# A gated linear attention with a mixture of experts behind it: the first place done in halves, and two edits to the loads and the order of step 0

## The chip, the cores and the metric

The kernel runs on one core of a Trainium2 chip. The core has a matrix engine (TensorE, PE in the profile, its weight loads PEld), a vector engine (VectorE, DVE), an engine for functions of single elements (ScalarE, ACT), a general one (GpSimd, POOL), and a queue engine (SyncE, SP) that here only issues DMA transfers. ScalarE and GpSimd issue some transfers too. Each engine takes its own instructions in order and waits for others by semaphores. The metric is the time of one execution on the device in microseconds.

## The reference

Inputs q, k, v and alpha have the shape (4 batches, 8 heads, 768 positions, 48). For each batch and head a state of 48 x 48 runs over the positions:

```
state = alpha_t[:, None] * state + k_t (outer) v_t
y_t   = q_t @ state
```

The outputs of all heads at one position are joined to a row x of 384 numbers (3072 rows). Then each row goes to the one of 8 experts with the largest logit:

```
logits = x @ w_gate;  e = argmax(logits);  g = softmax(logits)[e]
out    = g * (relu(x @ w1[e]) @ w2[e])          # w1[e]: 384 x 1024, w2[e]: 1024 x 384
```

All numbers are float32.

## The kernel before

**Places.** The positions are cut into 6 chunks of 128, and each chunk of each batch is a place: 24 places, place s being chunk s // 4 of batch s % 4. Within a place the running products of alpha are taken as exponentials of sums of logarithms. For a place s this happens:

- `load` (L401) issues the transfers of alpha, k, q and v for the place on SP's queue. At the start they go one by one, in the order of the strings in `singly` (L622): each letter is the next transfer of that input.
- `logs` (L411): ScalarE takes the logarithm of alpha (`lna`).
- `cums` (L427): TensorE multiplies `lna` with a triangular matrix, which gives the running sums in the PSUM bank `cum`; ScalarE takes two exponentials of them, `icp` (negative sign) and `cp`. For the two first places the second call takes the bank `x`.
- `operands` (L475): k times `icp` and q times `cp` go into one of three buffers `kqb`. GpSimd does this, and VectorE for place 0.
- `transposes` (L484): TensorE turns four pairs of heads of k, then of q; VectorE or ScalarE copies the result out as `kT` and `qT`.
- `scores` (L498): eight matmuls into the banks `sA` and `sB`.
- `mask` (L507): VectorE multiplies both banks with a causal mask (`dA`, `dB`).
- `attend` (L534): the masked scores with v into `y`; from chunk 1 on `read_state` adds the part of the state before it.
- `keys_values` (L543): k with v into another part of the banks of `y`; `add_state` (L561) copies it out as the batch's state.
- `result` (L555) copies y out as `yT`; `rows` (L570), `logits`, `gate` and `keep_rows` make the row of x, the gate and its weight, and write x to DRAM.
- `decay_out` (L443) sends one row of `cp` or `icp` to another tile with a small DMA, issued on ScalarE's queue.

**Order.** The order of all instructions is written out by hand: the loop over i from -4 to 23 (from L720) calls these functions for different places. Step i takes the scores of place i, the transposes of place i + 1, the operands of place i + 2, and the sums of places that `sums_to` (L612) lists: places 0 and 1 in step -2, places 2 and 3 in step 0, 4 and 5 in step 1, then one or two more per step, until they are five places ahead. The steps before 0 fill the pipeline: `operands(0)` in step -2, `transposes(0)` in step -1. In steps 0 to 2 the second sums stand between `attend` and `keys_values`.

Ahead of the loop, `idle(3)` (L637) issues three matmuls of zeros from the tile `er` whose results are not used.

PSUM has eight banks: two for `y`, two for `tp`, and one each for `cum`, `sA`, `sB` and `x`.

**Experts.** After the last step the rows are sorted to the experts, gathered by indirect DMA, and go through both layers, expert by expert, with weights loaded ahead. The change does not touch this part.

Of the kernel before, what the change touches and what calls it, by code (L numbers as in the profile page):

```python
# [8 lines left out]
F32 = mybir.dt.float32  # L9
# [5 lines left out]
AF = mybir.ActivationFunctionType  # L15
# [5 lines left out]
def kernel(  # L21
# [31 lines left out]
    C = 128  # L53
# [335 lines left out]
    with tc.tile_pool(name="ld", bufs=6) as ld, \  # L389
# [37 lines left out]
        def cums(s, bank="cum"):  # L427
            cum = ps.tile([C, 512], F32, name="cum", tag=bank)
            if s < APART:
                nc.tensor.matmul(cum[:, :Dm], lhsT=cum_m[:], rhs=st[s]["lna"][:], start=True, stop=True)  # L430
# [5 lines left out]
            nc.scalar.activation(icp[:], cum[:, :Dm], AF.Exp, scale=-1.0)  # L436
            nc.scalar.activation(cp[:], cum[:, :Dm], AF.Exp)
            st[s]["cp"], st[s]["icp"] = cp, icp
# [22 lines left out]
        def by_half(t):  # L461
            return t.rearrange("s p a d -> s a p d")[:, :, :, :D]
# [11 lines left out]
        def operands(s):  # L474
            d = st[s]  # L475
            kq = kqb[s % 3]
            eng = nc.gpsimd if s else nc.vector
            for i, n, e in ((0, "k", "icp"), (1, "q", "cp")):
                eng.tensor_tensor(  # L479
                    by_half(kq[:, i]), d[n].rearrange("s (a p) d -> s a p d", a=2),  # L480
                    d[e][:].rearrange("s (a p d) -> s a p d", a=2, p=NP), op=ALU.mult,
                )

        def transposes(s):  # L484
            d = st[s]
            for i, n in enumerate(("kT", "qT")):
                tp = ps.tile([C, NP, C], F32, name="tp", bufs=2)
                for p in range(NP):
                    nc.tensor.transpose(tp[:, p, :], pair(kqb[s % 3][:, i], p), ident[:])  # L489
                d[n] = work.tile([C, NP, C], F32, name=n)  # L490

                if 0 < s < B - 1 or i and s < NT - B - 2:
                    nc.vector.tensor_copy(d[n][:], tp[:])  # L493
                else:
                    nc.scalar.copy(d[n][:], tp[:])
# [109 lines left out]
        def do(f, i, *a):  # L605
            if 0 <= i < NT:
                f(i, *a)
# [12 lines left out]

        loaded = dict(a=0, k=0, q=0, v=0)

        singly = {-5: "aakq", -4: "kqav", -3: "akq", -2: "aav", -1: "kq", 0: "avakq", 1: "avkq", 2: "a"}

        def load_next(n, many):
            load(loaded[n], n, many)
# [2 lines left out]
        def loads_for(i):  # L629
            for n in singly.get(i, ""):  # L630
                load_next(n, 1)
            if i > 1:
                for n, upto in ("a", sums_to(i + 4 + (i > 3))), ("v", i + 3), ("k", i + 5), ("q", i + 5):
                    while loaded[n] <= min(upto, NT - 1):
                        load_next(n, 2)

        def idle(n):  # L637

            t = ps.tile([C, NP, C], F32, name="sA")
            for _ in range(n):  # L640
                nc.tensor.matmul(t[:, :2, :], lhsT=er[:, 0].rearrange("s a d -> s (a d)"), rhs=er[:, :2], start=True, stop=True)

        loads_for(-5)
        nc.vector.memset(er[:], 0.0)
        nc.gpsimd.memset(iw[:], 0.0)
        for i in range(2):
# [66 lines left out]
        for i in range(-4, NT):  # L713
            loads_for(i)
            do(scores, i)
            if i < NT - 1:
                do(result, i - 1)
            do(logits, i - 2)
            if i >= B:
                do(add_state, i - 1)  # L720
            do(gate, i - 2)
            if i > 0:
                for s in new_logs(i):
                    logs(s)
# [676 lines left out]
```

## Time and profile before

Three runs gave a median of 393.21 us (391.83 to 393.31). The profiled execution took 390.48 us; its span is 388.8 us at a granted clock of 0.998.

| | us |
|---|---|
| median of the runs | 393.21 |
| the profiled execution / its span | 390.48 / 388.8 |
| TensorE busy | 380.0 |
| ScalarE / VectorE / GpSimd busy | 230.2 / 210.4 / 149.7 |
| scores of step 0 / 1 begin | 8.95 / 14.08 |

How to read the profile: a timeline line has the start in us, the duration, the engine, the line of the kernel, the operation, what it writes and reads, and the number of instructions merged. In square brackets stands how long the engine was idle before it and what ended that. `SPq` and `ACTq` are DMA issues on these engines' queues. In the rows of digits each digit is the busy share, in tenths, of one fortieth of the span.

### The profile page before, as it was taken

The numbers are of one execution on the slowest core, as the hardware profiler recorded it, in microseconds if no ns is written. First come the engines' busy times: TensorE is split into PE (matmuls) and PEld (weight loads), VectorE is DVE, ScalarE is ACT, GpSimd is POOL, SyncE is SP. The second block draws the span as 40 slices with busy tenths as digits, with TensorE's granted clock in tenths as the row PEclk, the third lists the DMA queues.
The fourth block names the chain that finished last, engine by engine and source line by source line (L and its number), as shares of the span: only waits on it lengthen the run. The fifth ranks groups of instructions, "written<-read, shape, count | busy, mean of one in ns | idle before, by whom it ended". The sixth has DMA issues, their size and how long they took to land. (4 is left out here: it accounts for less than half of the span.)

```text
span 388.8 us, 9126 instructions
## 1 busy us (share of the span) xinstructions
PE 380.0 (98%) x3394; PEld 326.1 (84%) x3394; DVE 210.4 (54%) x649; ACT 230.2 (59%) x521; POOL 149.7 (39%) x203
## 2 busy tenths in 40 slices
PE   7999999999999999999999999999999999999995
PEld 4678888888888886899889979979979979979964
DVE  5554667676676666625843672582581582551200
ACT  4575777677665431545665775675765765763640
POOL 6557464789768203257050034025016012011032
PEclk9999999999999999999999999999999999999999
DMA  9999998998994315789959459758767966701211
GB/s 172 197 205 218 194 227 190 210 220 212 237 260 139 117 42 183 157 293 256 278 154 256 78 194 231 159 187 193 196 195 178 205 195 152 176 16 58 57 55 66
DMA packets 156546, 68.09 MB, mean 175 GB/s; under 512 B 139339, under 2 KB 150722, under 8 KB 156500
## 3 DMA queue, kind: packets, MB, share of 16 engines
q1 hardware_dynamic: 151396, 57.77, 63.2%
q0 software_dynamic: 3408, 9.64, 8.2%
q8 instruction: 28, 0.46, 0.5%
q10 hardware_dynamic: 1696, 0.08, 0.3%
q14 instruction: 18, 0.15, 0.1%
HBM read 49.00 MB, written 9.58 MB: 151 GB/s over the span
## 5 line engine op out<-in xcount | busy, mean ns | idle before, releaser
L1077 POOL DMA_INDIRECT out_dram<-zo,sp x25 | 26.0, 1041 | 136.5 <-ACT zo L1102 127.1
L479 POOL TENSOR_TENSOR kqb<-k_sb,icp 128x384 f32<-128x384 f32 x23 | 23.0, 1000 | 28.7 <-PE y L550 12.5
L1051 PE MATMUL tp<-h_sb,w 128*128 128x416 f32 (+5 forms) x96 | 33.9, 496 | 0.0
L502 PE MATMUL sA<-qT,kT 48*128 48x128 f32 x192 | 27.7, 284 | 0.9 <-DVE qT L493 0.9
L502 PE MATMUL sB<-qT,kT 48*128 48x128 f32 x192 | 27.7, 285 | 0.0
L372 POOL DMA_INDIRECT xg<-x_rows,gp x25 | 23.8, 953 | 10.0 <-issue 6.6
L489 PE MATMUL tp<-ident,kqb 128*128 128x128 f32 x192 | 26.4, 280 | 0.3 <-DVE kqb L479 0.3
L1051 PEld LDWEIGHTS tp<-h_sb,w 128*128 128x128 f32 x96 | 18.0, 190 | 10.3 <-issue 3.7
L502 PEld LDWEIGHTS sA<-qT,kT 48*128 48x128 f32 x192 | 23.1, 187 | 3.8 <-issue 1.1
L980 ACT ACTIVATE h_sb<-h_sb 128x208 f32<-128x208 f32 (+6 forms) x28 | 10.3, 366 | 25.3 <-DVE h_sb L192 24.5
L192 DVE TENSOR_TENSOR h_sb<-cum,u 128x208 f32<-128x208 f32 (+6 forms) x28 | 10.1, 360 | 27.2 <-PE cum L969 20.7
L479 POOL TENSOR_TENSOR kqb<-q_sb,cp 128x384 f32<-128x384 f32 x23 | 23.1, 1003 | 3.1 <-DMA q_sb<-in_q_dram 3.1
L192 DVE TENSOR_TENSOR h_sb<-sB,u 128x208 f32<-128x208 f32 (+6 forms) x28 | 10.1, 360 | 26.1 <-PE sB L969 18.7
L558 ACT COPY yT<-y 128x512 f32<-128x512 f32 x24 | 14.1, 586 | 16.5 <-PE y L550 9.1
L489 PEld LDWEIGHTS tp<-ident,kqb 128*128 128x128 f32 x192 | 20.5, 141 | 3.4 <-issue 0.8
L969 PE MATMUL tp<-xgT,w 128*128 128x208 f32 (+6 forms) x112 | 23.1, 329 | 0.0
L502 PEld LDWEIGHTS sB<-qT,kT 48*128 48x128 f32 x192 | 23.1, 187 | 0.0
L510 DVE TENSOR_TENSOR dA<-sA,cmask 128x512 f32<-128x512 f32 x24 | 16.5, 688 | 10.8 <-PE sB L502 10.6
L195 DVE TENSOR_TENSOR th<-h_sb,th 128x208 f32<-128x208 f32 (+5 forms) x48 | 17.3, 361 | 8.0 <-ACT h_sb L982 8.0
L881 ACT COPY xgT<-xt 128x768 uint16<-128x768 uint16 (+6 forms) x25 | 20.8, 922 | 0.5 <-DMA xt<-xh 0.5
L576 PE MATMUL x<-iw,yT 128*64 128x104 f32 x368 | 20.8, 255 | 0.1
L1102 ACT COPY zo<-zr 128x768 uint16<-128x768 uint16 (+2 forms) x20 | 19.9, 1052 | 0.0
(304 smaller groups left out, 1032.2 us busy)
## 6 DMA issues: line engine op xcount, KB each, us to landing
w<-in_moe_w_dram SPq DMA_DIRECT2D x14, 1536.0 KB, 7.9
x_rows<-xs SPq DMA_DIRECT2D x24, 192.0 KB, 3.7
v_sb<-in_v_dram SPq DMA_DIRECT2D x10, 384.0 KB, 4.8
k_sb<-in_k_dram SPq DMA_DIRECT2D x9, 384.0 KB, 6.3
q_sb<-in_q_dram SPq DMA_DIRECT2D x9, 384.0 KB, 5.9
a_sb<-in_alpha_dram SPq DMA_DIRECT2D x7, 384.0 KB, 4.3
a_sb<-in_alpha_dram SPq DMA_DIRECT2D x10, 192.0 KB, 3.7
w<-in_moe_w_dram SPq DMA_DIRECT2D x6, 256.0 KB, 3.7
```

The source lines that it names most:

```text
L192: eng.tensor_tensor(out, a, b, op=ALU.add)
L195: eng.tensor_tensor(out, a, b, op=ALU.subtract)
L372: nc.gpsimd.indirect_dma_start(out=g["xg"][:r, j, :], out_offset=None, in_=x_d[:, :], in_offset=bass.IndirectOffsetOnAxis(ap=g["gi"](j, r) ...
L479: eng.tensor_tensor(by_half(kq[:, i]), d[n].rearrange("s (a p) d -> s a p d", a=2), d[e][:].rearrange("s (a p d) -> s a p d", a=2, p=NP), ...
L489: nc.tensor.transpose(tp[:, p, :], pair(kqb[s % 3][:, i], p), ident[:])
L502: nc.tensor.matmul(t[:, p, :], lhsT=d["kT"][r : r + D, p, :], rhs=d["qT"][r : r + D, p, :], start=True, stop=True,)
L576: nc.tensor.matmul(d["x"][o : o + HC, m, : D2 + E], lhsT=d["yT"][:, m // 2, m % 2, o : o + HC], rhs=iw[:, m, :], start=True, stop=True,)
L881: nc.scalar.copy(to[:, :, :, j * C : j * C + r], g["xt"][:, j].rearrange("p (h a) t -> p h a t", h=2)[:, :, :, :r],)
L969: nc.tensor.matmul(out, lhsT=ops[n_][0], rhs=ops[n_][1], start=first and n_ == names[0], stop=True, skip_group_check=True,)
L1051: nc.tensor.matmul(d2[:, :n], lhsT=w2[:, f, 2 * C :], rhs=h[:, f, :n], start=(f == 0), stop=(f == FB - 1),)
L1077: ins = nc.gpsimd.indirect_dma_start(out=out[:, :], out_offset=bass.IndirectOffsetOnAxis(ap=g["si"](j, r), axis=0), in_=zo[:r], in_offset= ...
L1102: copy(zo[:r].bitcast(U16).rearrange("p (c h) -> p h c", h=2), g["zr"][:r, j].rearrange("p (h a) c -> p h (a c)", h=2),)
```

## The change

Place 0 gets a function of its own, `first_step`, called in step -2. It takes the sums of place 0 in two halves of 192 columns (pairs of heads 0 and 1, then 2 and 3) in the banks `cum` and `sB`, the sums of place 1 in `x`, the exponentials, the products with k and q, the transposes and the copies of place 0 by halves; `kT` is copied by ScalarE, `qT` by VectorE. The second half of q is turned in the bank `cum`. The exponential `icp` of place 1 stands ahead of the copies of `kT`, `cp` behind them. The calls for place 0 in `cums`, `operands` and `transposes` fall away.

`idle` issues two matmuls of 512 columns instead of three of 256, from a constant zero instead of `er`, and stands ahead of the memsets. In `singly` the string of step -2 has v of place 1 ahead of the sixth transfer of alpha instead of behind it. In step 0 `keys_values` stands ahead of the second sums.

```diff
-        singly = {..., -2: "aav", ...}
+        singly = {..., -2: "ava", ...}
...
         def idle(n):
-            t = ps.tile([C, NP, C], F32, name="sA")
+            t = ps.tile([C, NP * C], F32, name="sA")
+            z = nc.const_aps.tensor(0.0, (C, NP * C))
             for _ in range(n):
-                nc.tensor.matmul(t[:, :2, :], lhsT=er[:, 0].rearrange("s a d -> s (a d)"), rhs=er[:, :2], start=True, stop=True)
+                nc.tensor.matmul(t[:], lhsT=z[:, :C], rhs=z, start=True, stop=True)
+
+        def first_step():
+            d = st[0]
+            two = (slice(0, 2), slice(2, NP))
+            def heads(t, h):
+                return t.rearrange("s (a p d) -> s a p d", a=2, p=NP)[:, :, two[h]]
+            cum = [ps.tile([C, 512], F32, name=n)[:, : Dm // 2] for n in ("cum", "sB")]
+            for h in range(2):
+                nc.tensor.matmul(cum[h], lhsT=cum_m[:], rhs=heads(d["lna"][:], h), start=True, stop=True)
+            one = ps.tile([C, 512], F32, name="x")[:, :Dm]
+            nc.tensor.matmul(one, lhsT=cum_m[:], rhs=st[1]["lna"][:], start=True, stop=True)
...
+            for t, f in zip(by, (-1.0, 1.0)):
+                for h in range(2):
+                    nc.scalar.activation(t[h], cum[h], AF.Exp, scale=f)
...
+            for i, n in enumerate("kq"):
+                t = d[n + "T"] = work.tile([C, NP, C], F32, name=n + "T")
+                for h in range(2):
+                    if i and h:
+                        tp = ps.tile([C, NP, C], F32, name="cum")
+                    elif h == 0:
+                        tp = ps.tile([C, NP, C], F32, name="tp", bufs=2)
+                    tps.append((t[:, two[h]], tp[:, two[h]], nc.vector.tensor_copy if i else nc.scalar.copy))
+                    nc.vector.tensor_tensor(
+                        by_half(kqb[0][:, i])[:, :, two[h]], d[n].rearrange("s (a p) d -> s a p d", a=2)[:, :, two[h]],
+                        by[i][h], op=ALU.mult,
+                    )
+                    for p in range(2 * h, 2 * h + 2):
+                        nc.tensor.transpose(tp[:, p, :], pair(kqb[0][:, i], p), ident[:])
...
+            nc.scalar.activation(st[1]["icp"][:], one, AF.Exp, scale=-1.0)
+            for t, tp, copy in tps:
+                copy(t, tp)
+            nc.scalar.activation(st[1]["cp"][:], one, AF.Exp)
 
         loads_for(-5)
+        idle(2)
         nc.vector.memset(er[:], 0.0)
...
         first_consts()
-        idle(3)
...
         for i in range(-4, NT):
...
-            do(transposes, i + 1)
+            if i >= 0:
+                do(transposes, i + 1)
             sums = list(new_sums(i))
-            for s in sums[:1]:
-                cums(s)
-            if i < 0:
-                for s in sums[1:]:
-                    cums(s, "x")
+            if i == -2:
+                first_step()
+            else:
+                for s in sums[:1]:
+                    cums(s)
...
-            do(operands, i + 2)
+            if i > -2:
+                do(operands, i + 2)
...
+            if i == 0:
+                keys_values(i)
             if i >= 0 and sums[1:]:
                 cums(sums[1])
                 for s in sums:
                     decay_out(s, (0,) if i else (0, 1))
-            do(keys_values, i)
+            if i:
+                do(keys_values, i)
```

More of the change, by code (lines that the diff above doesn't have):

```diff
@@ L425, in low_part, with cums @@
             )
-        def cums(s, bank="cum"):
-            cum = ps.tile([C, 512], F32, name="cum", tag=bank)
+        def cums(s):
+            cum = ps.tile([C, 512], F32, name="cum")
             if s < APART:
@@ L476, in operands @@
             kq = kqb[s % 3]
-            eng = nc.gpsimd if s else nc.vector
             for i, n, e in ((0, "k", "icp"), (1, "q", "cp")):
-                eng.tensor_tensor(
+                nc.gpsimd.tensor_tensor(
                     by_half(kq[:, i]), d[n].rearrange("s (a p) d -> s a p d", a=2),
@@ L490, in transposes @@
                 d[n] = work.tile([C, NP, C], F32, name=n)
-                if 0 < s < B - 1 or i and s < NT - B - 2:
+                if s < B - 1 or i and s < NT - B - 2:
                     nc.vector.tensor_copy(d[n][:], tp[:])
@@ L621 @@
         loaded = dict(a=0, k=0, q=0, v=0)
-        singly = {-5: "aakq", -4: "kqav", -3: "akq", -2: "aav", -1: "kq", 0: "avakq", 1: "avkq", 2: "a"}
+        singly = {-5: "aakq", -4: "kqav", -3: "akq", -2: "ava", -1: "kq", 0: "avakq", 1: "avkq", 2: "a"}
         def load_next(n, many):
@@ L637, in idle @@
         def idle(n):
-            t = ps.tile([C, NP, C], F32, name="sA")
+            t = ps.tile([C, NP * C], F32, name="sA")
+            z = nc.const_aps.tensor(0.0, (C, NP * C))
             for _ in range(n):
-                nc.tensor.matmul(t[:, :2, :], lhsT=er[:, 0].rearrange("s a d -> s (a d)"), rhs=er[:, :2], start=True, stop=True)
+                nc.tensor.matmul(t[:], lhsT=z[:, :C], rhs=z, start=True, stop=True)
[9 more added lines that the diff above has]
+            nc.tensor.matmul(one, lhsT=cum_m[:], rhs=st[1]["lna"][:], start=True, stop=True)
+            icp, cp = (work.tile([C, Dm], F32, name=n, bufs=6) for n in ("icp", "cp"))
+            by = [icp.rearrange("s (h w) -> s h w", h=2)[:, h] for h in range(2)], [heads(cp[:], h) for h in range(2)]
+            for t, f in zip(by, (-1.0, 1.0)):
+                for h in range(2):
+                    nc.scalar.activation(t[h], cum[h], AF.Exp, scale=f)
+            d["icp"], d["cp"] = icp, cp
+            by[0][:] = [t.rearrange("s (a p d) -> s a p d", a=2, p=2) for t in by[0]]
+            tps = []
+            for i, n in enumerate("kq"):
[12 more added lines that the diff above has]
+                        nc.tensor.transpose(tp[:, p, :], pair(kqb[0][:, i], p), ident[:])
+            st[1]["icp"] = work.tile([C, Dm], F32, name="icp", bufs=6)
+            st[1]["cp"] = work.tile([C, Dm], F32, name="cp", bufs=6)
+            nc.scalar.activation(st[1]["icp"][:], one, AF.Exp, scale=-1.0)
+            for t, tp, copy in tps:
+                copy(t, tp)
+            nc.scalar.activation(st[1]["cp"][:], one, AF.Exp)
```

## The prediction

> **What bounds the kernel now.** I read the busy shares first, then TensorE's and ScalarE's timelines over the first 20 us, where the change lies, then the waits of TensorE behind that.
>
> ```profile
> PE 380.0 (98%) x3394; PEld 326.1 (84%) x3394; DVE 210.4 (54%) x649; ACT 230.2 (59%) x521; POOL 149.7 (39%) x203
> PE   7999999999999999999999999999999999999995
> DMA  9999998998994315789959459758767966701211
> ```
>
> TensorE is the bound of the whole span, apart from the first slice of 9.7 us; its list of waits between 25 and 120 us is empty. So a microsecond taken out of TensorE's path at the start moves everything behind it by as much, if the moved steps find their data. The second digit row warns of that: for the first 117 us the DMA engines are nearly always busy, and the first loads arrive one after another, about 0.9 us apart.
>
> The first step on ScalarE, then TensorE, from the timelines (start, length, engine, line, operation, and in brackets the idle time before it with what ended it):
>
> ```profile
> 4.97 0.52 ACT L413 ACTIVATE lna<-a_sb 128x384 f32<-128x384 f32 x1 [0.83 <-DMA a_sb<-in_alpha_dram]
> 5.40 0.48 ACT L436 ACTIVATE icp<-cum 128x384 f32<-128x384 f32 x1
> 11.30 0.52 ACT L413 ACTIVATE lna<-a_sb 128x384 f32<-128x384 f32 x1 [1.18 <-DMA a_sb<-in_alpha_dram]
> 11.81 0.49 ACT L436 ACTIVATE icp<-cum 128x384 f32<-128x384 f32 x1
> 12.20 0.48 ACT L437 ACTIVATE cp<-cum 128x384 f32<-128x384 f32 x1
> 13.69 0.49 ACT L436 ACTIVATE icp<-cum 128x384 f32<-128x384 f32 x1 [1.00 <-PE cum L430]
> 14.08 0.48 ACT L437 ACTIVATE cp<-cum 128x384 f32<-128x384 f32 x1
> 14.59 0.51 ACTq L450 DMA_DIRECT2D dec<-cp  x1
> 15.19 0.59 ACT L558 COPY yT<-y 128x512 f32<-128x512 f32 x1 [0.63 <-ACT cp L437]
> 15.68 0.94 ACT L413 ACTIVATE lna<-a_sb 128x384 f32<-128x384 f32 x2
> ```
>
> ```profile
> 6.80 0.56 DVE L479 TENSOR_TENSOR kqb<-q_sb,cp 128x384 f32<-128x384 f32 x1 [0.32 <-DMA q_sb<-in_q_dram]
> 8.11 0.69 DVE L493 COPY qT<-tp 128x512 f32<-128x512 f32 x1 [0.75 <-PE tp L489]
> 8.72 1.00 POOL L479 TENSOR_TENSOR kqb<-q_sb,cp 128x384 f32<-128x384 f32 x1
> 8.95 0.34 PE L502 MATMUL sA<-qT,kT 48*128 48x128 f32 x1 [0.88 <-DVE qT L493]
> 10.04 1.09 PE L489 MATMUL tp<-ident,kqb 128*128 128x128 f32 x8
> 10.97 0.81 PE L430 MATMUL cum<-lna,cum_m 128*128 128x384 f32 x2
> 12.74 0.91 PE L430 MATMUL cum<-lna,cum_m 128*128 128x384 f32 x2
> 13.58 0.56 PE L550 MATMUL y<-v_sb,kqb 128*48 128x48 f32 x16
> 16.26 0.91 PE L430 MATMUL cum<-lna,cum_m 128*128 128x384 f32 x2
> ```
>
> What to see: TensorE starts the scores of step 0 at 8.95, their weights at 8.92, and runs on without a gap worth naming. But two points of this path are tied to other clocks too. The second sums of step 0 (12.74) start 0.06 after `cp` of place 2 ends (12.68), and that goes back over `icp` (11.81) to the `lna` of place 3 at 11.30, which waited for the fourth alpha tile from DRAM: ScalarE takes both logarithms before it takes `icp`. And the sums of step 1 (16.26) start just after the first `lna` of 15.68 ends (16.19), which stands in ScalarE's queue behind the chain 13.69, 14.08, the DMA issue of 14.59 to 15.10, and `yT`. So TensorE, the alpha tile and ScalarE's queue arrive here almost together; an advance of one alone is not enough.
>
> **The change part by part.** Durations are of the profiled execution.
>
> Idle products: three of 256 columns become two of 512, and they no longer wait for the memset of `er` (1.52), so they begin about when the engines are released, 0.8 to 1.0. The rows show a 256-column pass begun every 0.43 us; four of 512 columns take 3.4 us and end near 4.3. `lna` of place 0 ends at 4.14, so its sums may begin 0.1 later than now (4.24). Cover: `icp` can't start before the `lna` of place 1, which waits for its tile until 4.97, lets it (5.40). Cost nothing; without that cover, 0.1.
>
> The Trainium skill ("TensorE: Matmul & The Clock Gate", Part 1) states that the array runs at half clock until about 3.4 us of sustained work. This trace agrees although its granted clock reads 1.00 throughout: the longest pass of the sums is 795 ns, the median 488. By the rule the earlier start makes the first sums quick (0.3 less); by the row of 4.97 it is worth nothing.
>
> Halves of place 0. Nearest rows for half tiles are the 128x208 operations, 0.36 on both VectorE and ScalarE, begun some 0.28 apart. The four half exponentials take ScalarE from 5.40 to about 6.5, where `icp` of place 1 starts as now (6.50; it needs its own sums, 5.55 + 0.91). The halves of `kT` follow at about 6.9 and 7.2, done by 7.6, and `cp` of place 1 comes after them, done by 7.95 instead of 7.36. Who waits for it: GpSimd's product of 8.72 (0.8 spare), and the two `dec` DMA issues on ScalarE's queue, now 7.36 to 9.05, which then end by about 9.2, ahead of the next `lna` (9.59, bound by its tile). Hidden. On VectorE the products with q can't start before q lands, 6.80: halves 6.80 to 7.16 and 7.08 to 7.44. Two transposes take 0.40 (0.116 apart, 0.28 the last), so the second pair is ready at 7.88. A 128x256 copy lies between the 128x192 one (0.35) and the 128x512 one (0.69): 0.42. `qT`: 7.64 to 8.06 and 7.98 to 8.40. The scores of the first two pairs need only the first half and start at 8.18, the rest (0.5 later) finds the second half there. Gain at this point 8.92 - 8.18 = 0.74.
>
> Does it last? The transposes of place 1 begin at 9.30; GpSimd's second product ends at 9.72, and by then the four k transposes (0.47) are just done: no loss. The sums of place 2 at 10.23 find their `lna` (10.11). Attend at 10.97 instead of 11.71 needs v of place 0: issued at 6.45, between alpha tiles that took 4.12 and 4.09, so landed at about 10.55. Keys' products with values, moved ahead, take 0.40 and end at 12.3. Then the second sums must wait for `cp` of place 2. Its chain starts with the same tile at 11.30; only the 0.51 from `lna` to `icp` shrinks to the 0.43 seen at 4.97 and 5.40, since the sums are now there: 12.66. TensorE idles 0.35. **Gain left: 0.08.**
>
> The moved products are a gain of their own: the scores of step 1 come straight after the sums, at 13.50 instead of 14.08, 0.58 ahead; the transposes there need GpSimd's product that ends at 14.34, and have it. But the sums of step 1 wait for `lna` of 15.68, and its whole chain hangs on the second sums, which moved by 0.08 alone. TensorE idles 0.6 and starts them at 16.18. What is late next is ScalarE's queue; what follows in steps 1 and 2 keeps its order.
>
> Swap of v and the sixth alpha tile on SP's queue: v of place 1 is issued at about 11.04 instead of 11.84, alpha the other way round. The k tile behind both, issued at 12.78, landed at 17.04; one transfer (0.9) before that is 16.1 for alpha. Its `lna` starts at 16.11 now, and `icp` behind it waits for sums until 17.20, so 0.6 is spare. v gets earlier and nothing waited for it. Nothing; if alpha landed 1.0 later than I estimate, 0.4 loss. Bounds 0 to +0.5; I take 0, since the neighbouring k tile gives it.
>
> Second sums later on the queue: `dec` issues and `yT` hang on their end, which stays. Operands of place 0 leave the loop; GpSimd's order is unchanged.
>
> Sum: -0.74 + 0.66 lost at the alpha tile, -0.58 + 0.58 lost at ScalarE's queue: **-0.1 us**. From both sides: 0.0 if ScalarE keeps its 0.51, and -0.84 if neither wait binds (0.74 and the 0.1 by which the second sums now wait after attend). The profiled execution took 390.48 (span 388.8), so 390.4. The runs shown have a median of 393.21 (391.83 to 393.31), 0.7% above it; the four executions together have a median of 392.5. I set the kernel before at 392.9, between the two medians: **392.8**.
>
> **Rivals.**
>
> A. As above, -0.1.
>
> B. The gain comes through: in the timed runs the alpha tile lands before 10.6, or ScalarE's queue has the slack that I deny it. For it: 0.7 us is less than one transfer, and arrivals may shift by that. Against: nothing issued before that tile has changed. -0.84, so 392.1: still within 0.5% (2.0 us), which is about what a measurement of this kernel can tell from no change.
>
> C. Slower: TensorE's clock stays low into step 0. The idle products end 0.1 sooner than now and start 0.6 sooner, and the stretch from 5 to 9 us is thin (0.81, 0.83, 0.84 and 0.12 busy in its four single microseconds). If the array ran at the pace of the idle passes through scores, transposes and first sums of step 0 (1.1 + 0.9 + 0.8), these would double: +2.8, less the 0.66 that waits at the alpha tile, +2.1, so 394.9. It is slower than before from 2.6 us of low-clock work on. Against: the thin stretch is as thin now, and the transposes of 10.04 run at full pace.
>
> D. The halves do not do what they say: `qT` waits for something else (ScalarE's `kT`, or the second half), and the scores start only 0.3 sooner. Then the alpha tile hides the difference: -0.1 again.
>
> E. A larger gain, 2.0 and more, has no row: all that the change touches ends by 16.3, and there TensorE was idle for less than 0.3 after 8.92.
>
> **How the numbers follow.** A and D 0.68, B 0.22, C 0.07, E 0.03. The executions shown differ by 0.7% without any change, so a median under A, B or D can fall by over 0.5% below 393.21: about 0.13 of 0.90, with E faster 0.15. Slower: C, and 0.03 by spread, 0.10. Same 0.75. The range runs from the lowest execution shown less 0.1 (390.4) to the highest plus half of C's price (394.4).
>
> **What would show it.** In the changed kernel's timeline: scores of step 0 at 8.0 to 8.4; `lna` still at about 11.3 by its DMA; `icp` directly behind it; TensorE idle for 0.2 to 0.5 ahead of the second sums, released by `cp`, and for about 0.6 ahead of the sums of step 1, released by `lna`; from there all steps 0.0 to 0.2 earlier, with their old period. B is right if the sums of step 1 start at 15.6 or before; C if passes of step 0 are as long as the idle ones. The prediction is wrong if the second sums start well before the `lna` of place 3 allows, or a wait appears in steps 2 to 7 that is not there now.

## The result, and the profile after

Over 22 runs of each kernel the changed one has a median of 392.56 us (391.1 to 393.95), the kernel before 392.76 (391.26 to 394.8). The ratio is 0.9997, with a 95% interval from 0.9981 to 1.0013. The forecast was 392.8 and no measurable difference, and that is what came out: 0.2 us between the medians, while executions of either kernel lie up to 3.5 us apart. The interval stands for -0.7 to +0.5 us, so it can't tell the forecast's -0.1 from no change at all.

The profiled execution of the changed kernel took 393.42 us (span 391.7), 2.9 more than the span shown before. That is no loss of the change, since both kernels show such executions, but where the 2.9 us arose can be read, and it is taken up below. The execution shown before, 390.48, was faster than all 22 timed runs of its kernel.

The busy shares and two digit rows from the changed kernel's page:

```profile
PE 381.3 (97%) x3394; PEld 326.1 (83%) x3394; DVE 210.6 (54%) x652; ACT 230.5 (59%) x524; POOL 149.1 (38%) x203
...
PE   8899999999999999999999999999999999999995
...
DMA  8999899999984315789949759868767965711211
```

TensorE's first slice rose from 7 to 8 tenths, and the second fell from 9 to 8. That is the result at a glance: the first step starts earlier, and the time comes back as idle time one slice later. The next two fences show where. TensorE's timeline of the changed kernel (start, length, engine, line, operation, and in brackets the idle time with what ended it):

```profile
8.22 0.34 PE L501 MATMUL sA<-qT,kT 48*128 48x128 f32 x1 [0.34 <-DVE qT L683]
...
9.31 1.25 PE L488 MATMUL tp<-ident,kqb 128*128 128x128 f32 x8
10.40 0.81 PE L430 MATMUL cum<-lna,cum_m 128*128 128x384 f32 x2
11.14 0.64 PE L538 MATMUL y<-dA,v_sb 128*48 128x128 f32 x8
...
12.05 0.53 PE L549 MATMUL y<-v_sb,kqb 128*48 128x48 f32 x16
12.70 0.91 PE L430 MATMUL cum<-lna,cum_m 128*128 128x384 f32 x2
13.54 0.37 PE L501 MATMUL sA<-qT,kT 48*128 48x128 f32 x1
...
16.75 0.91 PE L430 MATMUL cum<-lna,cum_m 128*128 128x384 f32 x2 [1.03 <-ACT lna L413]
```

The scores of step 0 start at 8.22 instead of 8.95. The second sums of step 0 start at 12.70 instead of 12.74. Of the 0.69 us between these two leads, 0.16 went in the transposes of place 1 (9.31 to 10.40), where GpSimd's product with q came late; 0.34 are the moved products, which now run ahead of the second sums, as the run with them alone measures below; the other 0.19 are a wait for `cp`. So the scores of step 1 (13.54 instead of 14.08) still have a lead of 0.54, and it goes at the sums of step 1, which start at 16.75 instead of 16.26. ScalarE's timeline of the changed kernel tells who holds both sums:

```profile
11.36 0.52 ACT L413 ACTIVATE lna<-a_sb 128x384 f32<-128x384 f32 x1 [1.50 <-DMA a_sb<-in_alpha_dram]
11.79 0.47 ACT L436 ACTIVATE icp<-cum 128x384 f32<-128x384 f32 x1
12.16 0.48 ACT L437 ACTIVATE cp<-cum 128x384 f32<-128x384 f32 x1
13.65 0.49 ACT L436 ACTIVATE icp<-cum 128x384 f32<-128x384 f32 x1 [1.00 <-PE cum L430]
...
14.03 0.48 ACT L437 ACTIVATE cp<-cum 128x384 f32<-128x384 f32 x1
14.55 1.10 ACTq L450 DMA_DIRECT2D dec<-cp  x1
15.69 0.58 ACT L557 COPY yT<-y 128x512 f32<-128x512 f32 x1 [1.17 <-DVE dA L509]
16.18 0.53 ACT L413 ACTIVATE lna<-a_sb 128x384 f32<-128x384 f32 x1
```

The fourth alpha tile still lands just before 11.36. `icp` follows directly now, `cp` ends at 12.64, and the second sums begin 0.06 later. Then the second `dec` issue takes 1.10 us (14.55 to 15.65), `yT` can't start before 15.69 nor the next `lna` before 16.18, and the sums of step 1 wait for that. (The bracket of `yT` names VectorE's `dA`, which `yT` doesn't read; in the second execution of this kernel `yT` ran at 15.71, while that `dA` ran from 15.34 to 16.03.) TensorE's waits in the changed kernel between 5 and 120 us (total, times, longest) give the price:

```profile
PE cum L430 <- ACT lna L413: 1.0, 1, 1.0
PE ep L470 <- POOL er L459: 0.5, 2, 0.3
PE x L575 <- ACT xs L600: 0.4, 1, 0.4
PE sA L501 <- DVE qT L683: 0.3, 1, 0.3
```

The sums of step 1 start 0.49 later than in the execution before, and the waits of 0.5 and 0.4 in steps 3 and 4 add to it. To follow such an advance through the steps, I use the start of VectorE's first mask (`dA`) in each step, in the profiled executions:

| Kernel | scores, step 0 | second sums, step 0 | sums, step 1 | mask, step 2 | mask, step 5 | mask, step 8 | from there to the span's end |
|---|---|---|---|---|---|---|---|
| before | 8.95 | 12.74 | 16.26 | 21.39 | 38.43 | 54.56 | 334.2 |
| changed | 8.22 | 12.70 | 16.75 | 21.89 | 39.32 | 55.85 | 335.9 |
| changed, executed again | 8.37 | 13.31 | 16.77 | 21.90 | 39.08 | 56.21 | 334.1 |
| halves only | 8.25 | 12.67 | 16.26 | 23.21 | 40.06 | 57.01 | 334.3 |
| products ahead only | 9.28 | 13.41 | 16.87 | 22.00 | 39.02 | 55.96 | 334.1 |
| no wait for the fourth tile | 8.55 | 12.69 | 16.15 | 21.28 | 38.81 | 54.96 | 334.5 |
| `dec` issues later | 8.17 | 12.60 | 15.46 | 21.66 | 38.94 | 56.18 | 335.7 |
| both later | 8.61 | 12.82 | 15.68 | 20.92 | 37.92 | 55.62 | 334.7 |
| three more idle products | 10.91 | 15.04 | 18.56 | 23.70 | 40.89 | 57.63 | 335.4 |
| before, no `dec` from step 3 | 9.17 | 12.97 | 16.48 | 21.61 | 38.61 | 54.75 | 335.1 |
| changed, no `dec` from step 3 | 8.37 | 12.68 | 16.20 | 21.43 | 39.07 | 55.22 | 335.9 |
| both later, no `dec` from step 3 | 8.41 | 12.62 | 15.48 | 20.88 | 37.91 | 55.07 | 336.0 |

The last column explains the rest of the long span. In six of the twelve executions it is 334.1 to 334.7. The four with 335.7 and more, the changed kernel's own among them, have waits of 1.0 to 1.7 us that come much later; here they are in TensorE's timeline of the changed kernel:

```profile
175.60 0.62 PE L1017 MATMUL sA<-t,s 128*128 128x208 f32 x2 [0.74 <-ACT p L959]
...
187.54 0.62 PE L1017 MATMUL x<-t,s 128*128 128x208 f32 x2 [0.78 <-ACT p L959]
```

Of the 2.9 us, 1.3 had arisen by step 8 and 1.5 at these two places; without them the column would read 334.4. A second execution of the same kernel has neither, so the spread between executions is partly made there, far behind the change.

### The profile page after: what moved, and what is told of

Same layout as the page of the kernel before. It is cut to its first block, busy times and chain, and to the rows that moved or that the text cites. A ratio compares the mean times of both kernels' runs of the same rounds, so it can differ in the third digit from the quotient of the medians.

```text
span 391.7 us, 9131 instructions
## 1 busy us (share of the span) xinstructions
PE 381.3 (97%) x3394; PEld 326.1 (83%) x3394; DVE 210.6 (54%) x652; ACT 230.5 (59%) x524; POOL 149.1 (38%) x203
## 5 line engine op out<-in xcount | busy, mean ns | idle before, releaser
L488 PE MATMUL tp<-ident,kqb 128*128 128x128 f32 x184 | 25.3, 280 | 0.0
L192 DVE TENSOR_TENSOR h_sb<-sB,u 128x208 f32<-128x208 f32 (+6 forms) x28 | 10.1, 359 | 26.0 <-PE sB L1017 18.6
L488 PEld LDWEIGHTS tp<-ident,kqb 128*128 128x128 f32 x184 | 19.7, 141 | 2.4 <-POOL kqb L478 0.2
```

The costliest lines, as they stand in the source:

```text
L192: eng.tensor_tensor(out, a, b, op=ALU.add)
```

## The experiments

My theory T was the prediction's: what the halves and the moved products win is lost at ScalarE, first at the chain from the fourth alpha tile, then at the queue with the `dec` issues. Rival B: the steps have slack, and the gain gets through, to be lost further on if at all. Rival F: the saturated DMA engines set the pace by when tiles land, whatever ScalarE does. Theory G, that ScalarE's later `dec` issues take the lead back, came up when the first two locks were open.

### Each part alone

The halves without the moved products (`e1_halves_only`), an edit of the changed kernel:

```diff
-            if i == 0:
-                keys_values(i)
             if i >= 0 and sums[1:]:
...
-            if i:
-                do(keys_values, i)
+            do(keys_values, i)
```

> The changed kernel with the keys' products of step 0 put back behind the second sums. Theory T (the gain of the first step is lost at ScalarE's chain from the alpha tile of place 3, and again at its DMA issues): scores of step 0 at 8.1 to 8.4, second sums of step 0 at 12.6 to 12.9 after an idle TensorE of 0.7 to 0.8 (the products no longer fill it), scores of step 1 at 13.9 to 14.1 as in the kernel before, sums of step 1 at 16.1 to 16.8 as in both kernels. Rival B (the tile and the queue have slack, and the gain is lost further on): second sums at 11.9 to 12.2 and sums of step 1 at 15.6.

The moved products without the halves (`e2_kv_only`), the same lines the other way round in the kernel before:

> The kernel before with the keys' products of step 0 put ahead of the second sums, and nothing else of the change. Theory T: attend ends at about 12.65, the products run to 13.05, so the second sums start at 13.0 to 13.1 instead of 12.74 and take ScalarE's chain with them: sums of step 1 at 16.5 or later (0.3 later than before), so this half of the change alone costs 0.2 to 0.4. Rival B: scores of step 1 at 13.9, sums of step 1 at 16.0 to 16.3, no loss.

The first gave 393.01 us, the second 391.95, the kernel before beside them 391.09, one run each, which at a spread of 3.5 us says nothing by itself. The steps say more. With the halves alone, the scores of step 0 started at 8.25, the second sums at 12.67 after a wait of 0.21 for `cp` (I had expected 0.7 to 0.8), the scores of step 1 at 14.01 and the sums of step 1 at 16.26: as T expected, and no gain at that point. Then came something that I had costed at nothing. The alpha tile of place 5, which the change puts behind v on SP's queue, was late. ScalarE's timeline of this kernel, and then TensorE's:

```profile
15.68 0.53 ACT L413 ACTIVATE lna<-a_sb 128x384 f32<-128x384 f32 x1
18.62 0.52 ACT L413 ACTIVATE lna<-a_sb 128x384 f32<-128x384 f32 x1 [2.41 <-DMA a_sb<-in_alpha_dram]
```

```profile
12.67 0.91 PE L430 MATMUL cum<-lna,cum_m 128*128 128x384 f32 x2 [0.21 <-ACT cp L437]
...
16.26 0.91 PE L430 MATMUL cum<-lna,cum_m 128*128 128x384 f32 x2
...
19.95 0.91 PE L430 MATMUL cum<-lna,cum_m 128*128 128x384 f32 x2 [1.76 <-ACT cp L437]
```

The second sums of step 1 lost 1.76 us to it. The prediction had put this swap at 0, with 0.5 as its upper bound.

With the moved products alone, this execution began 0.33 later (scores at 9.28, against 8.95; TensorE's clock came late, see the part on the clock), so I measure from one step to the next. The second sums start 1.37 after the first attend product (12.04 to 13.41), against 1.03 before (11.71 to 12.74): the products take 0.34 ahead of them. The sums of step 1 come at 16.87, after a wait of 0.43 for `lna`. So the moved products don't bring the sums of step 1 forward, which hang on the chain behind the second sums; they push that chain back.

### The two waits at ScalarE

Without the wait for the fourth alpha tile (`e3_no_tile3_wait`): the logarithm of place 3 is taken from the tile of place 2, so place 3 has wrong decays.

```diff
-            nc.scalar.activation(t[:], st[s]["a"].rearrange("s h d -> s (h d)"), AF.Ln)
+            nc.scalar.activation(t[:], st[2 if s == 3 else s]["a"].rearrange("s h d -> s (h d)"), AF.Ln)
```

> The changed kernel, but the logarithm of place 3 is taken from the alpha tile of place 2, so it waits for no transfer; the transfer itself stays. This leaves the output of places 3 and after in batch 3 of the first chunk wrong. Theory T: logarithm of place 3 right behind that of place 2, at 9.8 to 10.1 instead of 11.36; icp behind its sums at about 11.25, second sums at 12.4 to 12.5 (bound by the products then), 0.2 to 0.3 earlier than in the changed kernel; sums of step 1 earlier by as much at most, since the DMA issues still hold ScalarE. Rival B: second sums where they are, 12.6 to 12.8.

And the changed kernel as it is, beside it (`e4_after_again`):

> The changed kernel once more, for how far its start varies between executions. Theory T: scores of step 0 at 8.1 to 8.4, second sums at 12.6 to 12.9, sums of step 1 at 16.1 to 16.8, the exact time set by how long the second DMA issue of step 0 on ScalarE's queue takes (0.5 to 1.1). Rival B: the sums of step 1 at 15.6 to 15.8 in this execution, the profiled one having been an accident.

The first gave 391.32 us, the second 392.15, the kernel before 391.09. Without the tile both logarithms ran at 9.75, `icp` at 11.43, and the second sums started right after the products, at 12.69, without a wait. This start was 0.33 later than that of the changed kernel's profile; from the first attend product to the second sums it is 1.37 us against 1.56 there, and against 1.81 in the second execution of the changed kernel, whose fourth tile landed at 11.97 (second sums 13.31, wait 0.39). The wait is the tile's, and it is small: 0.19 and 0.44 in these two executions. The sums of step 1 still waited 0.43 for `lna` (16.15): the second lock was shut, as T has it.

Then the `dec` issues of step 0 behind the first exponentials of step 1 (`e5_dec_later`), five rounds:

```diff
                     cums(s)
+                if i == 1:
+                    for s in (2, 3):
+                        decay_out(s)
...
-                for s in sums:
-                    decay_out(s, (0,) if i else (0, 1))
+                for s in sums if i else ():
+                    decay_out(s, (0,))
```

> The changed kernel with the two decay DMA issues of step 0 moved behind the first two exponentials of step 1 on ScalarE's queue. Theory T: yT straight after cp of place 3 (at 14.5), logarithm of place 4 at 15.0 to 15.2 unless its alpha tile lands later (it is then released by a DMA, at 15.1 to 15.4), sums of step 1 at 15.6 to 16.0 instead of 16.75; all steps behind 0.5 to 1.0 earlier than in the changed kernel's profile, and 0.3 to 0.8 us less time, at the edge of what five rounds tell. Rival B (the queue does not hold the sums of step 1): sums of step 1 at 16.2 or later.

And with that the logarithm of place 3 behind `cp` of place 2 (`e6_both_later`):

```diff
                     cums(s)
+                if i == 0:
+                    logs(3)
...
-                for s in new_sums(i + 1):
+                for s in list(new_sums(i + 1))[: 1 if i == -1 else None]:
```

> As the one before, and the logarithm of place 3 moved behind cp of place 2 on ScalarE. Theory T: icp of place 2 right after its sums at 11.2 to 11.3, second sums of step 0 at 12.4 to 12.6, sums of step 1 at 15.5 to 15.9; 0.1 to 0.2 better than the one before, 0.4 to 1.0 us less than the kernel before. Rival B: as the changed kernel, 0.0.

The medians are 392.31 (391.17 to 393.58, 12 runs) and 392.58 (392.03 to 394.84, 12), against 393.04 for the kernel before (27 runs): ratios 0.999 [0.9971, 1.001] and 1.0 [0.998, 1.002]. Both locks open as T says: with the issues moved, `yT` ran at 14.30 and the sums of step 1 at 15.46 without a wait; with both moved, the second sums stand directly behind the products (12.82) and the sums of step 1 at 15.68. **Yet no fall of the time shows.** The intervals leave room for 1.1 and 0.8 us, so the times alone don't refute T's 0.3 to 1.0; the steps tell more. With `dec` later alone, the lead went at once, to the swapped alpha tile and to v (TensorE's timeline of that kernel):

```profile
15.46 0.82 PE L430 MATMUL cum<-lna,cum_m 128*128 128x384 f32 x2
16.62 0.65 PE L538 MATMUL y<-dA,v_sb 128*48 128x128 f32 x8 [0.34 <-DMA v_sb<-in_v_dram]
...
18.40 0.91 PE L430 MATMUL cum<-lna,cum_m 128*128 128x384 f32 x2 [0.69 <-ACT cp L437]
```

With both later the lead held through step 5 (37.92 against 38.43, while this execution had begun late), and was gone at step 6 (45.20 against 43.69). What stood there: TensorE waited 0.89 for GpSimd's product with q of place 6, and the pair of `dec` issues on ScalarE's queue took longer. The timelines of that kernel's GpSimd and of ScalarE's queue:

```profile
38.31 1.00 POOL L478 TENSOR_TENSOR kqb<-q_sb,cp 128x384 f32<-128x384 f32 x1 [2.37 <-ACT lna L413]
```

```profile
41.88 2.31 ACTq L450 DMA_DIRECT2D dec<-cp  x2
```

Before, that product ran at 35.39, and the pair took 1.19 from 41.26. Two suspects, then: late tiles (F), or the `dec` issues of steps 3 to 6, which hold ScalarE (G).

### Are delays passed through?

Three more idle products (`e7_idle5`), three rounds:

```diff
-        idle(2)
+        idle(5)
```

> The changed kernel with five idle products ahead of the first sums instead of two, which delays the first sums by some 2.6 to 3 us. It measures whether time at the start goes through to the end. Theory T (TensorE is the bound from step 1 on and has no slack): scores of step 0 at 10.3 to 11.0, sums of step 1 later by 1.3 to 2.2 than in the changed kernel, and the whole time longer by as much: 1.3 to 2.2 us. Rival F (the saturated DMA engines set the pace of the first 117 us, and TensorE's start has slack to catch up): sums of step 1 later, but the steps from 8 on at the same times, and the time within 0.5 us.

394.66 us (394.31 to 396.16, 8 runs), ratio 1.0052 [1.0031, 1.0074], which is 2.0 us of 393.04 (1.2 to 2.9). The scores of step 0 came 2.69 later than in the changed kernel, the second sums 2.34, the mask of step 2 1.81, that of step 8 1.78. Against the kernel before, whose time is the one compared, the scores came 1.96 later. A delay at the start passes through nearly whole. So the DMA engines do not set the pace on their own, as F would have it: a push back counts, a pull forward doesn't show.

### The `dec` issues of the later steps

First I moved the `dec` issues from step 3 on to SP's queue, in the kernel with both later (`e8_change_decay_on_sp`) and in the kernel before with the issues of step 0 later (`e9_before_decay_on_sp`):

```diff
-        def decay_out(s, which=(0, 1)):
+        def decay_out(s, which=(0, 1), eng=nc.scalar):
...
-                    nc.scalar.dma_start(decay[cc][b : b + 1, 1 - j, :], row)
+                    eng.dma_start(decay[cc][b : b + 1, 1 - j, :], row)
...
-                decay_out(sums[0])
+                decay_out(sums[0], eng=nc.sync if i > 2 else nc.scalar)
...
-                decay_out(i + 1, (1,))
+                decay_out(i + 1, (1,), nc.sync)
```

> The kernel with both waits of ScalarE's chain lifted (the decay issues of step 0 later, the logarithm of place 3 later), and from step 3 on the decay DMAs are issued on SP's queue, behind that step's store of x, instead of ScalarE's. Theory G (an advance of the start is taken back in steps 3 to 6, where two or three decay issues stand ahead of yT on ScalarE and take up to 2.3 us each pair while the DMA engines are full): yT of step 5 no longer at 43.4 to 44.2 but at 41.5 to 42.5, steps of 5.1 to 5.4 there, and 0.7 to 1.5 us less time than the kernel before. Rival F (the transfers themselves come too late for an earlier start, whoever issues): waits for k and q tiles of places 6 to 8 take the place of the issue, steps 5 to 7 still take over 6 in one place, and the time stays within 0.5 us of the kernel before.

> The kernel before (first step undivided, old order of loads and products) with the same two edits to the decay DMAs: those of step 0 behind the first exponentials of step 1, those from step 3 on SP's queue. The difference to the run before it is what the change is worth once ScalarE's queue is free. Theory T with G: sums of step 1 at 16.1 to 16.3 (bound by TensorE then), 0.3 to 0.7 us slower than the run before it, and faster than the kernel before by 0.3 to 0.8. Rival F: both runs alike within 0.2 us, and alike to the kernel before.

408.72 us (ratio 1.044 [1.0414, 1.0466]) and 407.34 (1.0413 [1.0393, 1.0433]), against 391.46: the experiment failed, by a mechanism of its own. SP's queue is full of loads and stores, and the `dec` rows came out of it late; TensorE waited 5.3 us once for ScalarE's `xs` and 2.4 once for `er`. It can't tell G from F. One reading is still sound, since until these waits start the two differ only by the change and by the later logarithm of place 3: the mask of step 2 stands at 20.51 and 21.20, that of step 5 at 37.40 and 38.05. The change with both locks open is worth 0.65 to 0.69 there, near the prediction's 0.74.

So I left those issues out instead: from step 3 on no `dec` row is sent, and the tile that they fill gets a constant, which makes the decays between blocks wrong. The three kernels are the one before (`e10_before_no_decay`), the changed one (`e11_change_no_decay`), and the one with both later (`e12_lifted_no_decay`), five rounds each:

```diff
-        def decay_out(s, which=(0, 1)):
+        def decay_out(s, which=(0, 1), leave=False):
...
+                        if leave:
+                            nc.gpsimd.memset(decay[cc][:], 1.04e-3)
-                    nc.scalar.dma_start(decay[cc][b : b + 1, 1 - j, :], row)
+                    if not leave:
+                        nc.scalar.dma_start(decay[cc][b : b + 1, 1 - j, :], row)
...
-                decay_out(sums[0])
+                decay_out(sums[0], leave=i > 2)
...
-                decay_out(i + 1, (1,))
+                decay_out(i + 1, (1,), True)
```

> The kernel before without the decay DMAs of places 8 and on and of the ends of chunks 1 and on (all that step 3 and later issue); a constant near their mean takes their place, so the carried state, and with it the rows of x and some of their experts, is only approximate. It frees ScalarE's queue from step 3 on without loading another queue. Base for the two runs beside it; also theory G (decay issues on ScalarE hold steps 3 to 6): no wait of TensorE between 28 and 60 us, steps of 5.1 to 5.4 after step 4. Rival F: a step of about 6 us there in this run too, from tiles that land late.

> The changed kernel with the same left out. Theory T: its gain is lost by the sums of step 1, so steps 2 to 8 are at the times of the run before it (0 to 0.5 later, by the tile that the second decay issue of step 0 waits for) and the time is the same within 0.5 us. Rival B/G alone (only the issues from step 3 on take the gain back): 0.4 to 0.8 us faster than the run before it.

> The changed kernel with its two waits of steps 0 and 1 lifted (decay issues of step 0 and the logarithm of place 3 later) and the same left out. Theory T with G: mask of step 2 at 20.4 to 21.0 instead of 21.4, the lead kept through step 8, and 0.4 to 0.8 us less time than the first run of the three. Rival F: the lead is gone by step 7 through waits for tiles, and the time is the same within 0.2 us.

| Kernel | median, us (12 runs) | ratio to the kernel before, 392.72 (29 runs) |
|---|---|---|
| before, no `dec` from step 3 | 391.41 (390.92 to 393.91) | 0.9978 [0.996, 0.9996] |
| changed, no `dec` from step 3 | 392.28 (391.13 to 394.3) | 0.999 [0.997, 1.001] |
| both later, no `dec` from step 3 | 391.45 (390.77 to 393.77) | 0.9975 [0.9956, 0.9994] |

If G held, the last would be ahead of the first by what the change wins. It isn't: 391.45 and 391.41. Leaving the issues out is worth about 0.2% in itself, but the change adds nothing that shows, within 0.7 us. The steps show the same course: against the first, the last is ahead by 0.73 at step 2 (20.88 and 21.61) and by 0.70 at step 5 (37.91 and 38.61), and behind at step 6 (44.37 and 44.05), with no `dec` issue left there. GpSimd's timeline, first of the kernel before without those issues, then of the one with both later:

```profile
34.68 1.00 POOL L482 TENSOR_TENSOR kqb<-k_sb,icp 128x384 f32<-128x384 f32 x1 [0.74 <-DMA k_sb<-in_k_dram]
36.80 1.00 POOL L482 TENSOR_TENSOR kqb<-q_sb,cp 128x384 f32<-128x384 f32 x1 [1.11 <-DMA q_sb<-in_q_dram]
```

```profile
34.67 1.01 POOL L481 TENSOR_TENSOR kqb<-k_sb,icp 128x384 f32<-128x384 f32 x1 [1.43 <-DMA k_sb<-in_k_dram]
38.21 1.00 POOL L481 TENSOR_TENSOR kqb<-q_sb,cp 128x384 f32<-128x384 f32 x1 [2.53 <-ACT lna L413]
```

In both the product with k ran at the same time, bound by its tile: on GpSimd the lead of 0.7 is already spent there. The product with q came 1.41 later, and TensorE waited 0.79 for it. G is rejected as what holds the lead, and F's mark, a lead gone by step 7 through a wait for a tile, came true.

What is it, then? The line names ScalarE's `lna`, but this product reads only `cp` of place 6 and the q tile of places 6 and 7. In the kernel before (35.39), in the kernel without the fourth tile's wait (37.97) and in the first of the two fences above, the same product is put down to that tile. The semaphore records in the traces settle it. A tile reports its landing in sixteen parts. In the kernel of the second fence fifteen parts had landed by 36.14 and the last at 38.07; in the kernel with both later by 36.20 and at 38.17. In both the product began 0.14 behind the last part, as it did in the kernel of the first fence (36.66). The first of two `lna` merely ended at the same moment.

So one part in sixteen was 1.9 us late. In the list of DMA queues a single packet marked `instruction` stands just there: of 16 KB, from 35.17 to 36.20 in the kernel of the second fence, from 35.50 to 36.46 in the one with both later, but from 37.27 in that of the first fence, behind the tile. The list of the second fence's kernel from 35 to 37 us (queue, kind, packets, MB, share of 16 engines):

```profile
q8 instruction: 1, 0.02, 3.2%
```

I count over the fourteen executions and the loads of tiles issued in their first 40 us. During 193 loads such a packet (8 or 16 KB) ran, and in 92 of these the last part came over 0.5 us behind the fifteenth; during the 276 others none ran, and it happened twice. The pair of `dec` issues in step 5 goes with it too: where the pair took 2.1 us and more, a 16 KB packet ran during it, and where it took 1.19, the packet began at most 0.2 before its end. That a fetch of instructions holds one of the sixteen DMA engines, and that it is chance which transfer it meets, fits all of this; no run moved such a packet, so it is likely and not shown.

## Why the prediction was right

**The mechanism.** The change does what it says. `qT` was predicted at 7.64 and 7.98 and ran at 7.65 and 7.99; the scores of step 0 were predicted at 8.18 and started at 8.22; the gain was 0.73 of the 0.74. Rival D (halves that don't do it) is out, and E found nothing.

**First lock.** "The second sums must wait for `cp` of place 2": predicted 12.66, measured 12.70, released by the chain from the fourth alpha tile. The run without that tile's wait removed it. The predicted idle time of 0.35 was shorter, 0.19, since the sums of place 2 came at 10.40 and not at 10.23: GpSimd's product with q ended at 9.85, because the product with k ahead of it waited for its own tile until 7.88. I had kept the old times of GpSimd here.

**Second lock.** The scores of step 1, predicted at 13.50, came at 13.54. The sums of step 1 waited for `lna`, as predicted; the size was off. I had 16.18, the profiled execution has 16.75, others 16.2 to 16.8. The term mis-sized was the second `dec` issue: 0.51 before, 1.10 here, 0.50 in the second execution of the same kernel. (That execution had 16.77 all the same, since its fourth alpha tile was 0.6 later.) The alpha tile of place 4, an earlier transfer on that issue's semaphore, is not the reason: it had landed at 14.44, before the issue began at 14.55, and in the changed kernel without the later issues it landed at 14.52 and the issue took 0.50. An `instruction` packet ran from 14.24 to 15.25, and in each of the eight other executions that have this issue in its old place such a packet came only behind it, and it took 0.50 to 0.57. That the packet is the reason is likely and not shown. Rival B's mark, 15.6 or before, was reached only when the issues were taken out of the way (15.46).

**The swap.** Costed at 0, with 0.5 as the bound, from a landing estimated at 16.1. Measured: between 16.3 and 17.1 in most executions, which cost up to 0.69, and 18.6 once, which cost 1.76; there fifteen of the tile's sixteen parts had landed by 16.71, and an `instruction` packet ran from 16.32 to 17.20. This is the step of the sum that was furthest off. It didn't decide the median, because the lead that it could eat was gone anyway.

**What I had not seen.** The prediction had two locks and said that behind them every step would come 0.0 to 0.2 earlier. With both locks open, the lead of 0.7 lives through step 5 and dies at step 6, and no median moves. There is at least a third lock, a tile that lands late in step 5. The row for it was on the page that I quoted, DMA engines busy nearly all of the first 117 us; I used it only for the first five tiles. The number would have been the same, for one reason more. And "a wait appears in steps 2 to 7 that is not there now" did come true (0.5 and 0.4): by the prediction's own sign its picture behind the two locks was wrong. The changed kernel's two profiled executions are 0.5 later at step 2 and 1.3 and 1.7 later at step 8, not 0.0 to 0.2 earlier, though against a single and fast execution of the kernel before. So the two locks account for the loss of the lead up to step 2, as forecast; that the time came out as forecast with what followed is luck. Nor does the number test much: B's -0.84 lies only just outside the interval of -0.7 to +0.5.

**The clock.** Rival C did not occur: the transposes and scores of step 0 ran at the old pace. The prediction also weighed whether earlier idle products make the first sums quick. TensorE's timeline of the changed kernel, first of the profiled execution, then of the second one:

```profile
4.38 0.85 PE L654 MATMUL cum<-lna,cum_m 128*128 128x192 f32 x2
5.02 0.63 PE L654 MATMUL sB<-lna,cum_m 128*128 128x192 f32 x2
5.71 0.91 PE L656 MATMUL x<-lna,cum_m 128*128 128x384 f32 x2
```

```profile
4.34 0.59 PE L654 MATMUL cum<-lna,cum_m 128*128 128x192 f32 x2
4.77 0.49 PE L654 MATMUL sB<-lna,cum_m 128*128 128x192 f32 x2
```

In the first a pair with 192 columns, begun 3.5 us after the first idle product (0.84), took 0.85, nearly as long as a pair with 384 columns a little later (0.91). In the second, after the same products, it took 0.59. The traces' record of the granted clock starts with its release, at 5.30 in the first and at 3.86 in the second (the profile's rows show 1.00 before that too); over the fourteen executions it came anywhere from 3.86 to 7.09. So the release doesn't hang on the start of the products alone. The rule that the prediction weighed ("TensorE: Matmul & The Clock Gate", Part 1 of the Trainium skill: half clock until about 3.4 us of sustained work) also says that the window of 3.4 us is free-running and doesn't start with the kernel, and the executions agree. Nothing came of it in these two executions, since the exponentials waited for the `lna` of place 1, as the row said. With the products ahead only, released at 7.09, the first sums ran till 7.29, the transposes stood behind them, and the scores came 0.33 later.

## What to carry to other kernels

Before a stage is started earlier, look for everything that meets there at nearly the same time: here TensorE, a tile's landing and ScalarE's queue stood within 0.1 us of each other, so an advance of one alone could win no more than that. Then look past the first two meeting points, for as long as the DMA engines are saturated: opening two locks moved the loss by four steps and the time by nothing that shows. A delay has no such protection: 2.7 us at the start cost 2.0 at the end. Look for `instruction` packets among the DMA queues before a late tile is put down to the order of the loads.

## What the runs showed of the hardware

A DMA issue on ScalarE's queue mostly takes 0.5 us, but the same issue took 0.50 and 1.10 in two executions of one kernel, and a pair of them took 1.19 to 2.40 in step 5. The copy `yT`, next in ScalarE's order, began 0.03 to 0.09 behind the issue's end in the timelines shown.

The last of a tile's sixteen parts landed over 0.5 us behind the others in 92 of the 193 loads into which an `instruction` packet fell, and in 2 of the 276 others, as counted above.

Where the `dec` rows were late, the granted clock fell with TensorE's waits. Busy time by stretch of the kernel with both later and `dec` on SP's queue: the stretch, its length, busy time and instructions of TensorE, weight loads, VectorE, ScalarE and GpSimd, then the granted clock, the DMA share and GB/s (TensorE waits from 41.0 to 46.3):

```profile
43.00:44.00 1.00, 0.00 (x0) 0.00 (x0) 0.00 (x0) 0.00 (x0) 0.29 (x1) 1.00 0.57 199
44.00:45.00 1.00, 0.00 (x0) 0.00 (x0) 0.00 (x0) 0.00 (x0) 0.76 (x1) 0.57 0.04 8
...
54.00:55.00 1.00, 1.00 (x24) 0.99 (x22) 0.00 (x0) 0.00 (x0) 0.00 (x0) 0.81 1.32 223
62.00:63.00 1.00, 0.28 (x6) 0.09 (x2) 0.00 (x0) 0.97 (x3) 0.39 (x1) 1.00 0.24 46
...
64.00:65.00 1.00, 0.29 (x3) 0.29 (x4) 0.00 (x0) 0.00 (x0) 0.66 (x1) 0.81 1.18 230
...
71.00:72.00 1.00, 1.00 (x26) 1.00 (x22) 0.00 (x0) 0.56 (x1) 0.45 (x1) 0.77 1.15 310
```

The clock halved about 3.1 us into the first wait (0.57 over the microsecond from 44, so at about 44.1) and came back at about 54.4, 8 us after the work had resumed. In the second wait, from 62.3 to 64.7, it fell at about 64.6, after 2.3 us, and came back at about 71.5, 6.8 us after the resumption. These four changes lie 10.2, 10.2 and 6.8 us apart, which is three, three and two times 3.4. In the kernel before with the same issues on SP's queue they came at 45.6, 52.4, 66.1 and 69.5, so two, four and one times 3.4 apart. In both executions the clock changed on a beat of 3.4 us, and not a fixed time after a wait began or ended.

The same part of the Trainium skill as above gives about 3.4 us both for the idle window that throttles and for the busy one that releases, and these runs agree with such windows: a release came after one or two whole ones of work. They add one thing: the window before the second fall, 61.2 to 64.6, was not idle throughout, since TensorE worked until 62.3.

By estimate some 15 us of work at half clock cost about 7.4, and with the 7.7 us of the two waits that makes 15.1, of the 15.9 by which this kernel's span (404.7) is longer than that of the kernel before (388.8). Rows of 1.5 KB that land late cost about twice the wait here.
